# Softcap attention and a maxout feed-forward on one core: the third quad left whole, another pairing of row halves, three tiles of exponentials, and a new written order

## The chip, the core and the metric

The kernel runs on one core of one Trainium2 chip. A core has five engines with a queue of instructions each: TensorE (PE, matrix products into the accumulator memory PSUM, with a separate stream PEld for its weight loads), ScalarE (ACT, functions by element), VectorE (DVE, elementwise work and copies), GpSimd (POOL, which here issues nearly all loads) and SyncE (SP, which issues the transposing copies and most stores). Engines wait for each other through semaphores; within one queue nothing overtakes. The metric is the time of one execution on the device in microseconds (us).

## The reference

Eight batches of twelve heads of attention over 448 tokens with head width 64; scores are squeezed by a tanh before the softmax. The heads' outputs are put side by side to 3584 tokens of 768 features, and go through two products, their maximum, and a third product.

```python
scores = scale * np.matmul(q, k.transpose(0, 1, 3, 2))      # (8, 12, 448, 448)
scores = cap * np.tanh(scores / cap)
scores = scores - np.max(scores, axis=-1, keepdims=True)
attn = np.exp(scores)
attn = attn / (np.sum(attn, axis=-1, keepdims=True) + 1e-09)
x = np.matmul(attn, v)                                       # then (3584, 768)
h1 = x @ w1                                                  # w1, w2: 768 x 1024
h2 = x @ w2
return np.maximum(h1, h2) @ w_out                            # w_out: 1024 x 768
```

## The kernel before, in words

**Attention by quads.** Four heads (two rows of two heads) make a quad; there are 24, three to a batch, numbered from 0. Rows are numbered 0 to 47, two to a quad. For a quad, PE makes the scores with the 448 keys on the partitions (three blocks of 128 keys, j = 0 to 2, for each row o and head h; step `S`, line 439) and the 64 left-over keys of all four heads together (step `L`, line 457). A score step fills one of two PSUM tiles z (`s0`, `s1`), two heads at a time; ACT takes it out with a tanh into a tile of exponentials in bf16 (steps `T`, line 448, and `TL`, line 463) and then applies the exponential in place, several blocks at a time (step `E`, line 470). Row 0 of a quad has its blocks in a tile `e0`, row 1 and the left-over keys in a tile `e1`; there are EB = 2 of each kind. PE multiplies exponentials with values (`VL` line 530 for the left-over keys, `V` line 540, two steps u of 12 matmuls) into one of the two PSUM tiles s. The sums over keys come from a product with ones (`Y`): for the first three quads straight from the exponentials (lines 498 and 500, 16 matmuls), for the others after DVE has added the blocks (`A` line 480, `B` line 485), with 4 matmuls (line 503). DVE inverts the sums (`Yi`, three steps, lines 510 to 516) and normalizes (`N`, lines 555 and 559) into xT, the transposed input of the feed-forward, which also frees the PSUM tile.

**Feed-forward.** max(a, b) = relu(a - b) + b, so the kernel uses wd = w1 - w2 (six DVE subtractions, step `sub`, line 324) and a premultiplied wm = w2 @ w_out, made on PE in 12 groups at the start (`W` and `WC` turn w2 first). For each batch stage 1 makes g = relu(x wd) in 8 groups of 6 matmuls (evicted by DVE, line 614), and stage 2 makes out = x wm + g w_out for blocks of 128 tokens in two halves of 384 columns, 14 matmuls a group (evicted at line 649 and stored from there). Groups are numbered in order: 12 of premultiplication, then batch by batch.

**Row halves.** A group's matmul over 128 rows is split into two of 64 rows; two groups x and y run side by side, x on rows 0 to 63 and y on rows 64 to 127 (step `M x y n`, line 583), and change places later. Before a group changes halves, DVE has to pass it on with an empty instruction that waits for its last matmul (step `H`, line 591), since both halves write the same PSUM bank. Where y or x is -1, the other half runs alone; where x = y, full matmuls are used (line 578), as in the whole end of the kernel. A group's PSUM bank is one of four (`O`), and is freed by its eviction (`ev`).

**Cut.** In before, quad 2 is divided by queries into 256 and 192 columns (`SPLIT = (2,)`), so there are 25 items of attention rather than 24 (items 2 and 3 are quad 2, item 4 is quad 3, and so on), and stage 1 of batch 0 is made in two passes of 8 groups, 256 and 192 columns wide.

**What sets the order.** Nothing is planned at build time: a text, ORDER, lists every step, and each engine gets its instructions in that order. So one list sets all five queues. Loads (`lk`, `lq`, `lv`, `lw1`, `lw2`, `lwo`, lines 278 to 321) go through POOL; `cr` (line 374) is the transposing copy of a quad's q and k on SP from quad 5 on (before that PE transposes the rows, `X`, and DVE copies them out, `XC`); `st` stores; `D b n` issues n matmuls on a zero tile that are never read (line 337).

Of the kernel before, what the change touches and what calls it, by code (L numbers as in the profile page):

```python
# [14 lines left out]
T 1 0; E 1 1 0 2; M 1 0 4; ev 1; lq 4 0; X 4 2; XC 4; ev 0; Y 0 1; Yi 0 1; lw2 1; W 3 0; WC 3; W 2 2; WC 2; lv 0 3;
VL 0 1; lv 0 0; lv 0 1; V 0 0; V 0 1; Yi 0 2; Yi 0 3; N 0 0; N 0 1; S 2 0 0; T 2 0; E 1 1 2 4; E 1 0 0 3; O 2 3;
O 3 1; M 2 3 8; H 3; H 2; lw2 2; W 4 0; W 5 2; WC 4; WC 5; M 3 2 8; ev 3; lv 2 2; lv 1 0; lq 5 0; lv 1 3; lk 5 0;
X 5 0; O 4 2; O 5 1; M 4 5 4; XC 5; L 2 0; TL 2; M 4 5 1; S 2 2 1; T 2 2; ev 2; lw1 0; sub 1 0; M 4 5 3; H 5; S 2 1 0;
T 2 1; E 2 1 0 2; sub 0 0; Y 1 0; Yi 1 1; H 4; Yi 1 2; Yi 1 3; lv 1 1; lv 1 2; VL 1 1; V 1 0; V 1 1; N 1 0; N 1 1;
S 3 0 0; T 3 0; E 2 1 2 4; M 5 4 8; ev 4; lwo 1 0; O 6 3; O 7 0; M 6 7 1; S 3 2 0; T 3 2; M 6 7 2; lwo 1 1; M 6 7 5;  # L20
H 6; H 7; S 3 1 1; T 3 1; lk 6 0; lq 6 0; X 6 2; XC 6; ev 5; L 3 0; TL 3; E 3 1 0 2; M 7 6 8; ev 7; S 4 1 1; O 8 2;
O 9 1; M 8 9 1; S 4 0 0; T 4 0; T 4 1; lw1 1; sub 2 0; M 8 9 7; H 9; H 8; S 4 2 0; T 4 2; E 4 0 0 3; sub 3 0; ev 6;
M 9 8 8; ev 9; lv 2 1; lk 7 0; lk 8 0; lq 7 0; lq 8 0; lv 2 0; X 8 0; XC 8; ev 8; X 7 3; XC 7; lv 2 3; VL 2 1; Y 2 1;
Yi 2 1; Yi 2 2; Yi 2 3; lw1 2; sub 4 0; lk 10 0; lk 10 1; lk 9 0; lq 9 0; lq 10 0; lk 11 0; lk 11 1; lq 11 0; lk 12 0;
cr 5; lk 12 1; lq 12 0; lv 3 1; lv 3 0; lk 13 0; lv 3 2; S 5 0 0; T 5 0; O 10 0; O 11 2; M 10 11 3; V 2 0; V 2 1;
N 2 0; L 4 0; M 10 11 5; H 10; H 11; E 3 1 2 4; Y 3 3; TL 4; N 2 1; M 11 10 1; S 4 5 0; T 4 5; lv 3 3; lk 13 1;
lq 13 0; cr 6; lv 4 0; lv 4 1; lv 4 2; lv 4 3; M 11 10 4; S 4 4 1; T 4 4; M 11 10 3; S 5 1 0; T 5 1; X 9 1; S 5 2 1;
T 5 2; sub 5 0; ev 10; Yi 3 1; Yi 3 2; ev 11; O 13 0; M 13 -1 2; O 14 3; M 13 14 4; Yi 3 3; H 13; S 4 3 0; T 4 3;
E 4 1 0 2; O 17 2; M 17 14 2; M 17 13 4; H 14; M 14 13 1; XC 9; A 4 0 1; H 17; M 14 13 1; ev 13; VL 3 1; V 3 0; V 3 1;
N 3 0; N 3 1; S 5 5 0; T 5 5; M 14 17 4; ev 14; O 15 1; M 15 17 2; O 19 0; M 15 19 4; H 15; lk 14 0; lk 14 1; lq 14 0;  # L30
lk 15 0; lk 15 1; lq 15 0; lv 5 0; lv 5 1; lv 5 2; lv 5 3; lk 16 0; lk 16 1; lq 16 0; lk 17 0; lk 17 1; L 5 1; cr 7;
A 4 1 1; O 12 3; M 12 19 2; H 19; M 12 15 3; ev 17; M 12 15 1; M 19 15 1; H 12; M 19 15 1; ev 15; S 5 3 0; M 19 12 4;
ev 19; M -1 12 1; O 18 2; M 18 12 1; O 16 1; M 18 16 1; ev 12; M 18 16 4; H 18; M -1 16 1; H 16; E 4 1 2 4; B 4 0;
B 4 1; A 4 1 2; TL 5; T 5 3; E 5 0 0 3; S 5 4 1; T 5 4; E 5 1 0 2; M -1 18 1; M 16 18 5; ev 18; A 4 0 2; O 22 0;
M 16 22 1; O 20 3; M 20 22 1; ev 16; A 5 0 1; M 20 22 5; VL 4 0; V 4 0; V 4 1; Y 4 2; Yi 4 1; Yi 4 2; Yi 4 3;
M 20 22 2; L 6 1; TL 6; M 20 22 5; H 22; O 21 1; M 20 21 1; M -1 21 1; M 22 21 4; S 6 5 1; M 22 21 8; N 4 0; N 4 1;
# [700 lines left out]
```

## Time and profile before

| | us |
|---|---|
| time, median of 3 runs (329.39 to 330.75) | 329.54 |
| the profiled execution, whole | 329.36 |
| its span | 327.6 |
| PE busy | 318.0 |
| ACT busy | 273.3 |
| DVE busy | 244.8 |
| first matmul starts | 0.99 |
| first tanh starts | 6.33 |
| last tanh or exponential ends | 288.0 |
| last matmul ends (last eviction begins) | 323.4 |

The busy time of PE is the union of its matmuls, whose ends are modelled, so a busy PE may still wait for less than a matmul's length. Durations below are taken by starts where instructions follow each other.

### The profile page before, as it was taken

The page shows a single profiled execution, that of the slowest core. Times are in us where ns is not written, and L with a number is a line of the kernel's source. Part 1 is how long each engine was busy: PE and PEld are TensorE (multiplying, and loading weights), DVE is VectorE, ACT ScalarE, POOL GpSimd, SP SyncE. Part 2 cuts the span into 40 slices and gives each one's busy share as a digit, 9 for nine tenths or more (in the row PEclk, how much of TensorE's full clock was granted, in tenths as well). Part 3 has the DMA queues.
Part 4 walks back from the last instruction along what each step waited for, and adds up shares of the span by engine and source line. Part 5 has one row for each costly group of instructions (what it writes and reads, how often), then busy time and mean ns, then how long its engine had stood idle before and what let it go on. Part 6 is the DMA issues. An engine that isn't in the chain of part 4 may idle for free.

```text
span 327.6 us, 10011 instructions
## 1 busy us (share of the span) xinstructions
PE 318.0 (97%) x4288; PEld 195.1 (60%) x4288; DVE 244.8 (75%) x446; ACT 273.3 (83%) x244; POOL 164.2 (50%) x243
## 2 busy tenths in 40 slices
PE   7699999999999999999999999999999999999994
PEld 6455567576555655655665565675567667655552
DVE  2339798989877887987888778878789775995422
ACT  4998999999999999999999998999899988710000
POOL 8546699997796885565576386542202000000000
PEclk9799999999999999999999999999999999999999
DMA  8999999999999999999999999995953042004006
GB/s 152 199 223 234 270 187 159 154 173 196 169 155 183 152 125 185 184 133 165 148 193 118 145 151 212 161 87 95 189 123 46 2 115 79 3 2 144 2 0 192
DMA packets 135083, 45.90 MB, mean 140 GB/s; under 512 B 116224, under 2 KB 130688, under 8 KB 134656
## 3 DMA queue, kind: packets, MB, share of 16 engines
q0 software_dynamic: 95456, 25.08, 76.7%
q1 hardware_dynamic: 39040, 19.18, 29.7%
q10 hardware_dynamic: 544, 1.02, 0.9%
q8 instruction: 33, 0.54, 0.7%
q14 instruction: 10, 0.08, 0.1%
HBM read 47.45 MB, written 11.01 MB: 178 GB/s over the span
## 4 chain that ended last, share of the span: by engine, by line
PE 89%; ACT 8%; issue 1%; DVE 0%; DVEq 0%
PE mm L583 56%; PE s L540 8%; PE mm L578 8%; PE s L439 8%; ACT e L448 5%; ACT e L470 3%; PE s L530 2%; PE s L457 2%; PE mm L503 1%; PE mm L337 1%; PE mm L366 1%; PE mm L498 1%; PE mm L345 1%; ACT e L463 0%; DVE qkT L371 0%
## 5 line engine op out<-in xcount | busy, mean ns | idle before, releaser
L470 ACT ACTIVATE e<-e 128x1792 bf16<-128x1792 bf16 (+4 forms) x73 | 140.7, 1937 | 0.3
L448 ACT ACTIVATE e<-s 128x896 bf16<-128x896 f32 (+2 forms) x144 | 123.9, 933 | 10.7 <-PE s L439 10.6
L583 PE MATMUL mm<-wo_sb,gT 64*128 64x384 bf16 x768 | 96.2, 323 | 0.0
L583 PE MATMUL mm<-xT,wd_sb 64*128 64x448 bf16 (+2 forms) x768 | 80.1, 326 | 0.0
L583 PE MATMUL mm<-wm_sb,xT 64*128 64x384 bf16 x576 | 77.2, 323 | 0.0
L583 PEld LDWEIGHTS <-gT 64*128 64x128 bf16 x768 | 49.0, 94 | 22.6 <-issue 2.4
L303 POOL DMA_DIRECT2D vp<-in_v_dram x48 | 30.4, 637 | 61.1 <-PE mm L503 30.0
L583 PEld LDWEIGHTS <-wd_sb 64*128 64x128 bf16 x768 | 46.7, 94 | 19.8 <-issue 2.9
L285 POOL DMA_DIRECT2D kqs<-in_k_dram x76 | 54.5, 720 | 6.7 <-DMA vp<-in_v_dram 4.2
L439 PE MATMUL s<-qkT 64*128 64x448 bf16 (+2 forms) x300 | 53.7, 346 | 2.9 <-ACT e L448 1.6
L583 PEld LDWEIGHTS <-xT 64*128 64x128 bf16 x576 | 38.9, 94 | 16.6 <-issue 2.2
L614 DVE TENSOR_SCALAR gT<-mm 128x448 bf16<-128x448 f32 (+2 forms) x72 | 39.2, 567 | 10.2 <-PE mm L583 5.6
L649 DVE COPY osb<-mm 128x384 f32<-128x384 f32 x54 | 29.2, 552 | 19.3 <-PE mm L578 10.4
L285 POOL DMA_DIRECT2D kqs<-in_q_dram x38 | 34.9, 920 | 3.1 <-DMA vp<-in_v_dram 1.5
L540 PE MATMUL s<-e,vp 128*32 128x448 bf16 (+2 forms) x600 | 32.5, 347 | 0.0
L303 POOL DMA_DIRECT2D vl<-in_v_dram x48 | 29.2, 617 | 5.4 <-DMA gT<-in_moe_w_dram 4.1
L559 DVE TENSOR_TENSOR xT<-s,inv 64x448 bf16<-64x448 f32 (+2 forms) x50 | 30.2, 604 | 2.2 <-PE mm L583 1.2
L439 PEld LDWEIGHTS <-qkT 64*128 64x128 bf16 x300 | 20.8, 94 | 17.4 <-issue 5.3
L480 DVE TENSOR_TENSOR esum<-e 128x896 bf16<-128x896 bf16 x42 | 25.6, 616 | 4.9 <-PE mm L583 2.7
L485 DVE TENSOR_TENSOR esum<-esum,e 64x896 bf16<-64x896 bf16 x42 | 26.0, 619 | 3.1 <-PE mm L583 1.4
L480 DVE TENSOR_TENSOR esum<-esum,e 128x896 bf16<-128x896 bf16 x42 | 25.5, 622 | 3.1 <-PE mm L583 2.1
L463 ACT ACTIVATE e<-s 128x896 bf16<-128x896 f32 (+2 forms) x25 | 22.5, 900 | 0.8 <-PE s L457 0.4
(54 smaller groups left out, 254.5 us busy)
## 6 DMA issues: line engine op xcount, KB each, us to landing
out_dram<-osb SPq DMA_DIRECT2D x51, 192.0 KB, 4.3
vp<-in_v_dram POOLq DMA_DIRECT2D x38, 160.0 KB, 4.8
kqs<-in_q_dram POOLq DMA_DIRECT2D x47, 112.0 KB, 5.4
kqs<-in_k_dram POOLq DMA_DIRECT2D x76, 56.0 KB, 4.7
osb<-in_moe_w_dram POOLq DMA_DIRECT2D x2, 1024.0 KB, 9.0
gT<-in_moe_w_dram POOLq DMA_DIRECT2D x3, 512.0 KB, 9.8
wo_sb<-in_moe_w_out_dram POOLq DMA_DIRECT2D x4, 384.0 KB, 7.6
w1l<-in_moe_w_dram POOLq DMA_DIRECT2D x1, 1024.0 KB, 5.4
```

The lines of the kernel that those rows point to most:

```text
L285: nc.gpsimd.dma_start(out=to, in_=x)
L303: nc.gpsimd.dma_start(out=to, in_=x)
L439: nc.tensor.matmul(ps[:, h, x * w : (x + 1) * w], k_of(t, o, h, j), q_of(n, o, h))
L448: nc.scalar.activation(e, slots[n, s][:, :, :m], AF.Tanh, scale=scale / cap)
L470: nc.scalar.activation(e[:, j0 * m : hi], e[:, j0 * m : hi], AF.Exp, scale=float(cap))
L480: nc.vector.tensor_add(d, e[:, 0:2, :] if j == 1 else d, e[:, 2 * j : 2 * j + 2, :])
L540: nc.tensor.matmul(vals[n][R32[m], u, :w], vp[t % VB][:, x, j if turned_by_pe(t) else 2 * j, u::2], e_of(n, o, h, j), start=False, stop=(j ...
L559: nc.vector.tensor_mul(x[to], vals[n][r, 1, :w], sums[n, 3][to, :w])
L578: nc.tensor.matmul(self.ps, w, x, start=first, stop=self.at[0] == self.n)
L583: ins = nc.tensor.matmul(self.ps, w[r], x[r], start=first, stop=self.at == [self.n, self.n]).ins
L614: nc.vector.tensor_relu(gT[b // 2][:, f, cs], ps)
L649: nc.vector.tensor_copy(o[:, hs], ps)
```

## The change

Two constants and the order. SPLIT is empty, so quad 2 is treated as the others, with items numbered like quads, and stage 1 of batch 0 has 8 groups of 448 columns; its groups are numbered 12 to 25 rather than 12 to 33. EB is 3: three tiles e0 and three tiles e1. ORDER is another text throughout: other loads first, other pairs of groups, other places for every step. The number of `D` matmuls goes from 48 to 80. The functions are unchanged; all line numbers are six lower.

```diff
-    EB = 2
+    EB = 3
-    SPLIT = (2,)
+    SPLIT = ()
```

The order's first part, before and after (the rest differs as much):

```diff
-ld0 k; ld0 q; dm; ms0; D 0 32; cd k; cd q; lq 3 0; id; Xh 0 0 1; XC 0 0; Xh 0 1 0; XC 0 1; ms; S 0 2 0; T 0 2;
-S 0 0 1; T 0 0; S 0 1 0; T 0 1; E 0 0 0 3; lk 1 0; lq 1 0; lq 2 0; X 1 2; XC 1; S 0 3 1; S 0 4 0; T 0 4; T 0 3;
...
+lq 1 0; ld0 k; lk 1 0; dm; ms0; cd k; lw2 0; D 0 32; id; Xh 0 0 0; XC 0 0; ld0 q; cd q; Xh 0 1 1; XC 0 1; ms; S 0 1 0;
+T 0 1; S 0 0 1; T 0 0; S 0 2 0; T 0 2; E 0 0 0 3; X 1 2; XC 1; S 0 4 1; T 0 4; S 0 3 0; T 0 3; E 0 1 0 2; D 3 8;
+W 1 3; D 0 8; L 0 1; TL 0; S 0 5 0; T 0 5; E 0 1 2 4; W 0 0; lv 2 3; lv 0 2; lv 0 3; lk 3 0; lwo 0 0; lq 2 0; lv 3 3;
+lk 2 0; X 2 1; WC 0; XC 2; lq 3 0; X 3 2; XC 3; S 1 1 1; T 1 1; S 1 0 0; D 0 8; T 1 0; lk 4 0; lq 4 0; X 4 0; D 1 8;
+L 1 1; TL 1; XC 4; S 2 0 0; T 2 0; lw2 1; W 2 1; WC 1; WC 2; S 1 4 1; T 1 4; Y 0 2; S 2 2 0; T 2 2; D 0 8; S 2 1 1;
+T 2 1; O 0 0; O 1 3; M 0 1 3; S 1 3 0; T 1 3; E 1 1 0 2; M 0 1 1; lwo 0 1; M 0 1 4; Yi 0 1; H 1; S 1 5 1; T 1 5;
+W 3 1; S 1 2 0; T 1 2; E 1 1 2 4; E 1 0 0 3; H 0; M 1 0 8; WC 3; O 2 2; O 3 1; M 2 3 3; ev 0; ev 1; M 2 3 5; H 2;
+lw2 2; lk 5 0; lv 1 2; lv 1 0; lq 5 0; lv 1 1; X 5 0; XC 5; W 4 3; WC 4; Yi 0 2; VL 0 1; S 2 5 0; T 2 5; lv 0 0;
+lv 0 1; lk 6 0; V 0 0; V 0 1; Yi 0 3; N 0 0; N 0 1; H 3; W 5 0; WC 5; D 3 8; Y 1 3; Yi 1 1; Yi 1 2; E 2 0 0 3;
+S 2 4 0; M 3 2 3; S 2 3 1; T 2 3; M 3 2 5; ev 2; ev 3; O 4 0; O 5 3; M 4 5 8; lk 9 0; lq 8 0; lq 6 0; X 6 2; lk 10 0;
+lw1 0; sub 1 0; L 2 1; T 2 4; E 2 1 0 2; TL 2; E 2 1 2 4; lv 1 3; VL 1 0; V 1 0; V 1 1; H 5; H 4; XC 6; Yi 1 3; N 1 0;
+N 1 1; M 5 4 8; lwo 1 0; lk 8 0; ev 4; O 6 1; O 7 2; M 6 7 1; S 3 0 1; T 3 0; M 6 7 3; S 3 2 0; T 3 2; lwo 1 1;
+M 6 7 4; ev 5; H 6; H 7; lk 7 0; lq 7 0; X 7 0; XC 7; lw1 2; sub 5 0; lq 9 0; S 3 1 1; T 3 1; lw1 1; lk 10 1; lq 10 0;
+lk 11 0; lv 3 2; lk 11 1; lq 11 0; lv 2 0; lv 2 2; cr 5; lk 12 0; lv 2 1; lk 12 1; lq 12 0; lk 13 0; lk 13 1; lq 13 0;
+lv 4 0; lv 4 1; lv 4 2; lv 4 3; lv 3 1; lv 3 0; lk 14 0; lk 14 1; M 7 6 5; S 3 5 0; T 3 5; M 7 6 3; ev 6; L 3 1; cr 6;
+TL 3; sub 0 0; X 9 3; XC 9; ev 7; S 3 3 0; T 3 3; O 8 0; O 9 1; M 8 9 3; S 3 4 1; T 3 4; M 8 9 5; H 8; H 9; S 4 4 0;
+T 4 4; sub 2 0; X 8 3; XC 8; sub 4 0; S 4 3 1; T 4 3; M 9 8 2; S 4 5 0; T 4 5; M 9 8 5; S 4 2 1; T 4 2; M 9 8 1; ev 9;
+ev 8; sub 3 0; O 10 2; O 11 3; M 10 11 8; Y 2 1; H 11; H 10; lq 14 0; lk 15 0; lk 15 1; lq 15 0; lv 5 0; lv 5 1;
+lv 5 2; L 4 0; cr 7; VL 2 1; Yi 2 1; Yi 2 2; Yi 2 3; V 2 0; V 2 1; N 2 0; N 2 1; lv 5 3; lk 16 0; lk 16 1; lq 16 0;
+lk 17 0; lk 17 1; lq 17 0; lv 6 0; M 11 10 8; ev 11; O 12 0; O 15 1; M 12 15 6; H 12; H 15; ev 10; E 3 1 0 2;
```

In before the three thirds of w1 (`lw1 0`, `lw1 1`, `lw1 2`) are asked for as POOL's loads 23, 30 and 38; in after `lw1 0` is load 30, `lw1 2` load 37 and `lw1 1` load 39. On SP, quads 13 and 14, and 21 and 22, change places.

More of the change, by code (lines that the diff above doesn't have):

```diff
@@ L15 @@
[L15 to L24, printed above, removed]
@@ new lines @@
+S 6 0 0; T 6 0; ev 17; M 21 22 2; ev 19; M 21 22 1; O 23 3; M 21 23 1; S 5 0 1; T 5 0; A 4 1 2; M 21 23 1; H 22;
+M 22 23 3; S 5 2 0; T 5 2; E 5 1 0 2; M 22 23 2; VL 4 1; B 4 0; B 4 1; Y 4 0; V 4 0; V 4 1; Yi 4 1; Yi 4 2; H 21;
+Yi 4 3; S 6 1 0; T 6 1; M 22 23 6; A 5 1 1; N 4 0; M 22 23 1; M 22 21 1; H 23; M 22 21 1; S 6 5 0; N 4 1; ev 22;
+M 23 21 12; O 20 0; M 23 20 2; O 25 1; M 25 20 1; S 6 4 1; M 25 20 3; E 5 0 0 3; ev 21; A 5 0 1; A 5 0 2; T 6 5;
+E 5 1 2 4; T 6 4; M 25 20 8; O 24 2; M 25 24 1; H 20; S 6 2 0; T 6 2; E 6 0 0 3; B 5 1; A 5 1 2; M 25 24 1; M 20 24 4;
@@ new lines @@
+O 26 3; M 26 32 4; H 32; A 6 1 1; O 31 0; M 26 31 2; H 26; M 32 31 1; B 6 0; M 32 31 3; M 32 26 1; H 31; B 6 1;
+M 32 26 1; ev 32; S 8 3 1; T 8 3; M 31 26 3; S 8 1 0; T 8 1; E 7 1 0 2; M 31 26 1; A 6 1 2; M 31 -1 1; O 33 1;
+M 31 33 1; O 30 2; M 30 33 1; ev 31; ev 26; M 30 33 2; lv 6 1; lv 6 2; lv 6 3; VL 6 1; lk 18 0; lk 18 1; lq 18 0;
+L 8 0; TL 8; lk 19 0; lk 19 1; lq 19 0; cr 9; E 7 0 0 3; Y 6 0; Yi 6 1; Yi 6 2; Yi 6 3; V 6 0; V 6 1; M 30 33 2;
+M 30 -1 1; H 33; H 30; S 8 0 0; T 8 0; E 7 1 2 4; N 6 0; N 6 1; A 7 1 1; M 33 -1 1; M 33 30 5; O 34 3; M 34 30 1;
@@ new lines @@
+VL 8 0; lv 10 3; lk 26 0; lk 26 1; lq 26 0; lk 27 0; lk 27 1; lq 27 0; lv 11 0; lv 11 1; lv 11 2; lv 11 3; lk 28 0;
+lk 28 1; lq 28 0; lk 29 0; Y 8 3; Yi 8 1; Yi 8 2; V 8 0; V 8 1; TL 11; Yi 8 3; N 8 0; N 8 1; lk 29 1; lq 29 0;
+lv 12 0; lv 12 1; lv 12 2; lv 12 3; lk 30 0; lk 30 1; M 36 37 1; O 40 1; M 36 40 12; H 36; S 11 5 1; O 44 3;
+M 44 40 2; M 44 36 1; ev 37; H 40; E 9 1 0 2; A 9 1 1; T 11 5; M 44 36 3; M 40 36 1; S 11 0 0; M 40 36 1; S 10 5 1;
+A 9 0 1; A 9 0 2; H 44; E 9 1 2 4; A 9 1 2; T 11 0; T 10 5; M 40 36 8; ev 36; st 1 4; M 40 44 4; ev 40; O 42 2;
@@ new lines @@
+ev 45; A 10 1 1; M 43 49 1; S 11 4 1; T 11 4; E 10 1 2 4; M 43 49 3; ev 43; O 53 3; M 53 49 1; S 12 1 0; T 12 1;
+M 53 49 1; O 51 0; M 53 51 1; ev 49; M 53 51 1; S 12 2 1; T 12 2; E 11 1 0 2; M 53 51 9; A 10 0 2; M 53 51 1; O 52 2;
+M 52 51 2; VL 10 0; V 10 0; V 10 1; B 10 1; B 10 0; A 10 1 2; Y 10 1; S 12 0 1; T 12 0; H 53; M 52 53 12; H 51;
+Yi 10 1; M 51 53 2; E 11 1 2 4; E 11 0 0 3; S 12 3 1; T 12 3; E 12 1 0 2; E 12 0 0 3; Yi 10 2; Yi 10 3; A 11 1 1;
+H 52; M 51 52 2; cr 14; st 1 6; ev 53; N 10 0; N 10 1; M 51 52 10; st 1 3; ev 51; O 55 1; M 55 52 2; O 54 3;
@@ new lines @@
+M 61 62 5; ev 62; A 13 0 1; O 66 2; M 61 66 1; O 68 1; M 68 66 2; ev 61; A 13 1 1; B 13 0; S 14 3 1; T 14 3;
+M 68 66 4; S 14 0 0; T 14 0; M -1 66 1; M 68 66 2; S 14 4 1; T 14 4; M 68 66 4; H 66; S 15 5 0; T 15 5; O 64 3;
+M 68 64 2; A 13 0 2; H 68; M 66 64 1; B 13 1; A 13 1 2; M 66 64 2; S 15 2 1; T 15 2; M 66 64 3; S 14 2 0; T 14 2;
+E 14 0 0 3; M 66 64 6; M 66 68 2; ev 66; lv 13 2; lv 13 3; VL 13 1; lk 32 0; lk 32 1; lq 32 0; L 14 0; TL 14; Y 13 0;
+Yi 13 1; H 64; Yi 13 2; Yi 13 3; V 13 0; V 13 1; N 13 0; N 13 1; M 64 68 12; ev 68; S 15 4 0; O 70 2; M 64 70 2;
@@ new lines @@
+ev 64; O 71 0; M 71 70 3; E 14 1 0 2; A 14 1 1; T 15 4; S 15 0 1; T 15 0; M 71 70 3; S 15 1 0; T 15 1; M 71 70 6;
+H 70; A 14 0 1; A 14 0 2; O 69 1; M 71 69 2; lk 33 0; lk 33 1; lq 33 0; lv 14 0; L 15 1; cr 16; L 16 0; lv 14 1;
+lv 14 2; lv 14 3; lk 34 0; lk 34 1; lq 34 0; lk 35 0; lk 35 1; lq 35 0; cr 17; lv 15 0; lv 15 1; lv 15 2; lv 15 3;
+lk 36 0; lk 36 1; lq 36 0; lk 37 0; lk 37 1; lq 37 0; lv 16 0; E 14 1 2 4; A 14 1 2; H 71; TL 16; TL 15; M 70 69 12;
+H 69; S 16 3 0; T 16 3; M 70 71 2; M 69 71 2; S 15 3 1; T 15 3; E 15 0 0 3; M 69 71 3; VL 14 0; B 14 0; B 14 1;
@@ new lines @@
+M 79 76 2; O 73 2; M 79 73 1; H 76; E 16 1 0 2; T 17 5; E 16 1 2 4; N 15 1; M 79 73 1; S 17 1 1; T 17 1; M 76 73 4;
+O 78 3; M 76 78 2; S 18 1 0; T 18 1; H 73; M 73 78 3; S 18 2 1; T 18 2; M 73 78 1; ev 76; H 79; M 73 79 1; H 78;
+M 73 79 1; S 17 3 0; T 17 3; M 78 79 3; S 18 5 1; T 18 5; M 78 79 1; O 83 0; M 78 83 1; A 16 0 1; ev 73; A 16 1 1;
+B 16 1; M 78 83 1; ev 78; O 84 2; M 84 83 1; ev 79; S 17 0 0; T 17 0; M 84 83 4; S 17 2 1; T 17 2; E 17 0 0 3;
+M 84 83 2; A 16 1 2; A 16 0 2; M 84 83 5; H 83; B 16 0; O 82 3; M 84 82 2; H 84; L 18 0; TL 18; VL 16 1; V 16 0;
@@ new lines @@
+O 114 0; M 114 115 2; O 110 3; M 114 110 1; A 23 0 2; ev 115; M 114 110 11; H 114; O 113 1; M 113 110 2; M 113 114 12;
+E 23 1 2 4; A 23 1 2; B 23 1; H 110; M 110 114 2; B 23 0; N 22 1; VL 23 0; H 113; Y 23 2; Yi 23 1; Yi 23 2; Yi 23 3;
+V 23 0; V 23 1; N 23 0; N 23 1; M 110 113 4; M -1 113 2; M 110 113 8; ev 110; st 6 0; O 116 2; M 116 116 6; ev 116;
+ev 113; O 117 3; M 117 117 6; O 118 2; M 118 118 6; ev 117; ev 118; O 119 1; M 119 119 6; ev 119; O 120 3;
+M 120 120 6; ev 120; O 121 2; M 121 121 6; O 122 1; M 122 122 6; ev 122; O 123 3; M 123 123 6; ev 121; ev 123;
```

222 lines of the change are left out of this document (84 added, 138 removed).

## The prediction

> **What bounds the kernel now.** Five views, in this order. First the page: busy shares, and the slices.
>
> ```profile
> PE 318.0 (97%) x4288; PEld 195.1 (60%) x4288; DVE 244.8 (75%) x446; ACT 273.3 (83%) x244; POOL 164.2 (50%) x243
> ...
> PE   7699999999999999999999999999999999999994
> ...
> PEclk9799999999999999999999999999999999999999
> ...
> PE 89%; ACT 8%; issue 1%; DVE 0%; DVEq 0%
> ```
>
> PE is the bound from the third slice on; ACT's 8% of the chain can only lie early. Second, stretches of the span (engine sums, clock, DMA):
>
> ```profile
> 5.26:8.68 3.42, 1.65 (x42) 0.96 (x38) 1.40 (x7) 2.35 (x3) 3.42 (x6) 1.00 1.26 191
> 8.68:12.09 3.41, 3.15 (x67) 2.36 (x68) 1.38 (x3) 3.38 (x4) 1.96 (x5) 0.50 1.11 186
> 12.09:17.00 4.91, 2.96 (x41) 1.93 (x40) 1.36 (x3) 4.88 (x7) 2.03 (x4) 1.00 1.27 209
> 17.00:31.50 14.50, 14.28 (x249) 8.37 (x248) 9.32 (x17) 13.33 (x13) 8.58 (x15) 1.00 1.21 226
> 31.50:50.00 18.50, 18.50 (x362) 11.14 (x358) 16.43 (x27) 17.82 (x19) 14.05 (x21) 1.00 1.41 225
> ```
>
> PE idles visibly only before 17 us. ACT starts at 6.33 and is full from then on. Third, ACT's waits:
>
> ```profile
> ACT e L448 <- PE s L439: 10.6, 15, 1.9
> ```
>
> Those are waits for scores; none is for a tile of exponentials. Fourth, the longest piece of the chain (start, us), and four rows of PE's timeline, for the price of a matmul:
>
> ```profile
> 296.02 27.40 PE mm L578 x160
> ```
>
> ```profile
> 54.02 1.26 PE L583 MATMUL mm<-xT,wd_sb 64*128 64x256 bf16 x20
> 55.20 0.38 PE L457 MATMUL s<-qkT 64*32 64x448 bf16 x8
> ...
> 69.99 1.88 PE L583 MATMUL mm<-xT,wd_sb 64*128 64x192 bf16 x36
> 71.87 0.37 PE L439 MATMUL s<-qkT 64*128 64x448 bf16 x2
> ```
>
> The 160 matmuls of the end (48 of 448 columns, 84 of 384, 14 of 512, 14 of 256: 64,512 columns) take 27.40 us, 0.425 ns a column. Below, a slot is one full matmul, or a pair on the two row halves; by starts in the timeline it costs 0.189 us at 448 columns, 0.163 at 384, 0.110 at 256, 0.087 at 192. The rows above show the short ones dearer in place: 18 pairs of 192 in 1.88 us (0.104), 10 of 256 in 1.18 (0.118). A half alone (-1 in a step) costs a whole slot. Fifth, where before stood at two moments:
>
> ```profile
> 32.26 0.75 PE L498 MATMUL mm<-e,ones 128*32 128x448 bf16 x12
> ...
> 323.44 0.42 DVE osb L652
> ```
>
> By slots the order before holds 311.6 us of PE work, 23.9 of it ahead of the sums of quad 1 (32.26). So PE, which starts at 0.99, idled 7.35 us before that point, and 323.44 - 32.26 - 287.7 = 3.5 us after it: 2.2 until 74.0 us (the second values of quad 4, with 63.5 us of slots ahead of them) and 1.3 in the 249 us that follow. Little is left to gain after 74. Around the work: 4.1 us from the last matmul's end to the span's end, and 1.8 between the span and the execution's 329.36 us, which lies 0.2 under the median of 329.54.
>
> **The change, part by part.**
>
> *No cut.* Stage 1 of batch 0 loses 45 pairs of 256, 45 of 192, one and three mixed with 384, and 8 lone halves; it gains 48 pairs of 448 and two of 384: 45 x 0.110 + 45 x 0.087 + 4 x 0.163 + 5 x 0.110 + 3 x 0.087 = 10.3 against 48 x 0.189 + 2 x 0.163 = 9.4, so 0.9 less. The attention of that quad has the same columns in fewer matmuls: 0.13 less over scores, sums and values. On ACT six tanh of 0.80 to 1.02 become six of 0.93, 0.1 less in all: nothing. DVE loses eight evictions (8 x 0.42 + 8 x 0.36 = 6.1 become 8 x 0.62 = 5.0) and one chain of sums.
>
> *New pairs.* Lone halves fall from 24 to 16, those eight being the cut's, counted above; pairs of unequal width from 49 to 45, likewise. The rest is renumbering: nothing, and hidden by nothing, as the slots are the same.
>
> *Three tiles of each kind.* No ACT wait was for one, so by itself 0; it only permits the order. A loss would need the second tile to have been free later, which a third cannot cause; a gain is bounded by ACT's 10.6 us of waits, nearly all after 130 us, when PE is the bound anyway.
>
> *The new order, to 32 us.* Warm matmuls go from 48 to 80. Eight cost 0.55 us on the chain, so +2.2 (no less than 1.8, at 56 ns each as the transposes of w2 run). They stand where PE waits for ACT: two score tiles, each freed only by its tanh. The first point that pins PE is the sums of quad 1 (Y 1), which need its last exponentials. Ahead of those ACT has 15 tanh x 0.81, 2 leftover tanh x 0.81 and two quads of exponentials (2.4 + 1.6 + 1.6 each): 25.0 us. From 6.33, and with 0.25 for what the same sum misses before (it gives 24.2 with a gap of 0.75, the trace 24.46), Y 1 can start at 31.6. Ahead of it PE has 23.4 us of slots, 6.9 of them warm: idle 31.6 - 0.99 - 23.4 = 7.2, as before. Behind it 289.35 us remain; before, at the same instant, 288.4 remained. So the new order is 1.0 us behind there, although its useful work is 1.05 less in all.
>
> *From 32 to 74 us.* Before idles 2.2. Of that the short pairs' excess over the prices used is 45 x 0.017 + 45 x 0.008 = 1.1, which goes. New: stage 1 of batch 0 can't begin on 256 columns; its fifth pair waits for xT of the whole third quad. PE gets there at 31.6 + 46.1 - 23.4 + 0.3 = 54.6. DVE, from the copy of row 7's transposes (42.1), has five subtractions (1.22), two copies (0.62), four wm evictions (0.55), the inversion (0.65 + 0.24 + 0.65) and the normalization (0.62 + 1.24): 12.9, so xT at 55.0, and with 0.2 for the handover PE waits 0.6. Idle here 2.2 - 1.1 + 0.6 = 1.7 (bounds 0 and 2.8).
>
> *Loads.* Weights of w1 move behind more rows. POOL waited until 37.73 for the second third of w1 when 12.4 MB of source had been asked for, 0.37 MB/us from 4.0 on. In the new order the last two thirds complete 13.7 and 14.95 MB: 41 and 44.4 us, needed at 42.1 and 46.4. Cost 0 with 1 to 2 us of cover; without it each us late is a us on xT above. Eight loads in flight, as before. At the start two row loads and a third of w2 are now issued ahead of the identity on POOL (0.57 us each, from 1.24): identity at 3.3 us, needed at 4.5, so 0. The SP queue has the same 19 transposes; quads 13/14 and 21/22 swap there, each still a quad ahead of its scores by the chain's 11 us a quad: 0.
>
> *From 74 us on.* Idle stays 1.3: nothing in the trace separates the orders there (bounds 0.7 and 2). The last 27.4 us are the same matmuls.
>
> Sum: 31.6 + 289.35 + 1.7 + 1.3 = 323.95, plus 4.1 and 1.8: 329.85, half a us over the profiled execution; I take 329.8, the median plus 0.3.
>
> **Clock.** The granted clock was 0.50 for 3.41 us after a stretch with PE busy 1.65 of 3.42, and stayed at 1.00 after one busy 2.96 of 4.91. In the new order the stretch 12 to 17 us holds 3.1 us of slots (leftover and two scores, half of w2, rows 2 and 3, 8 warm), about as before, so no second half-rate stretch is in the sum. *TensorE: Matmul & The Clock Gate* of the Trainium skill, section "What's actually happening", says that the array's clock is gated to half by default and after an idle window of about 3.4 us; by that rule, the 3.41 us row agrees, a late load at 14 us would bring a second such window.
>
> **Rivals.** (1) *Faster: the idle of 32 to 74 us was the cut's altogether.* For it: H handovers come every 6 short pairs, every 0.5 us; against it: xT's wait is new. Idle there 0, and 1.0 later: 31.6 + 289.35 + 1.0 + 5.9 = 327.85. (2) *Slower: w1 lands late.* Its thirds took 8.0 and 10.1 us to land before; the new order issues two of them close together. The 5 subtractions stand in front of the inversion of quad 2 on DVE, and all PE work left is stage 1. From 46.4 each us costs one; at 48.5 the time is 329.8 + 2.1 = 331.9, and past 1.4 us late it is slower by 0.5%. Against it: the 0.37 MB/us held over 33 us. (3) *A second window at half clock* between 12 and 19 us: up to 3.41/2 = 1.7 us of PE, of which the 7.2 us idle absorb half: 330.7. (4) *The third tile and the order do nothing*: 329.5; inside the forecast's range.
>
> **How the numbers follow.** Forecast with (4) 0.56, its own range 328.6 to 330.9; (1) 0.17; (2) 0.20; (3) 0.07. 0.5% is 1.65 us, about what a measurement of this kernel can tell: the bounds are 327.9 and 331.2. Faster: most of (1) and a little of the forecast, 0.15. Slower: (2), some of (3) and the forecast's edge, 0.23. Same 0.62. The range, from (1) to (2): 327.6 to 332.0.
>
> **What would show it.** PE matmuls 4156; the sums of quad 1 starting within 0.4 us of 31.6 (earlier: the pin is wrong); first 448-wide stage-1 pairs near 54, with a gap of about 0.6 after four pairs; idle later near 3 us; ACT ending between 286 and 291; the end stretch again 27.4 us. DVE waiting on a DMA into osb or w1l between 42 and 50 would be rival 2; a clock row under 1 after 12 us rival 3. A PE wait on qkT from SP, which I cost at nothing, would break the forecast.

## The result and the profile after

The changed kernel takes 337.08 us in the median of five runs (331.77 to 337.29), before 329.54 (329.32 to 330.75, five runs): 7.5 us or 2.3% more by the medians. The interval given for the ratio, 1.0107 (1.0061 to 1.0153), goes by the two shortest of the five runs alone, 331.77 and 335.02; only one of the other three was traced, so what made these two shorter is not shown. The profiled execution took 337.09 with a span of 335.3, as three of the five did. The forecast was 329.8, with a range to 332.0: wrong by 7.3 us against this execution, and the median of the five lies outside the range.

The page of the changed kernel: busy time, PE and its clock by slices of 8.4 us, and the chain by engine.

```profile
PE 321.5 (96%) x4156; PEld 188.3 (56%) x4156; DVE 243.9 (73%) x432; ACT 275.1 (82%) x242; POOL 164.4 (49%) x243
...
PE   7789999999995999999999999999999999999994
...
PEclk9799999999997899999999999999999999999998
...
PE 85%; ACT 6%; DMA 4%; DVE 3%; issue 1%; DVEq 0%
```

PE is still the bound, but slice 13 (100.6 to 109.0 us) is half empty, the clock row has a dip there that before has not, and the chain holds 4% of DMA, where before it held none. Stretches around that place, first after, then before (length, busy us of PE, PEld, DVE, ACT, POOL, granted clock, DMA share, GB/s):

```profile
99.00:102.55 3.55, 3.55 (x41) 2.67 (x39) 3.12 (x6) 3.55 (x4) 1.38 (x2) 1.00 1.71 165
102.55:104.91 2.36, 0.33 (x4) 0.00 (x0) 1.51 (x3) 2.36 (x3) 0.65 (x1) 1.00 1.97 109
104.91:111.74 6.83, 5.12 (x32) 2.43 (x34) 2.40 (x4) 3.32 (x3) 4.89 (x8) 0.50 1.47 151
111.74:116.00 4.26, 4.26 (x70) 1.96 (x68) 2.96 (x6) 2.60 (x3) 3.01 (x4) 1.00 1.83 171
```

```profile
104.91:111.74 6.83, 6.83 (x104) 4.02 (x106) 5.52 (x11) 6.83 (x5) 5.96 (x10) 1.00 1.79 162
```

In the same 6.83 us before issued 104 matmuls, after 32. PE's timeline and the chain show what PE waited for:

```profile
102.23 0.65 PE L577 MATMUL mm<-wo_sb,gT 64*128 64x384 bf16 x5
106.62 0.56 PE L433 MATMUL s<-qkT 64*128 64x448 bf16 x2 [3.75 <-DMA qkT<-kqs]
```

```profile
92.72 0.33 PE mm L577 x4
93.05 13.53 DMA qkT<-kqs
106.58 0.05 issue
106.62 0.56 PE s L433 x2
```

The first scores of quad 9 (step `S 9 5 0`) wait for the transposing copy of that quad. It is issued at 93.05 and lands 13.5 us later, at 106.58. SP's timeline of after shows what stands ahead of it, and of the two copies behind it:

```profile
83.30 9.46 SPq L624 DMA_DIRECT2D out_dram<-osb  x6
93.05 16.05 SPq L368 DMA_TRANSPOSE qkT<-kqs  x3
```

Those six are the stores of batch 0 (tile 1 at 83.3; tiles 2 and 0, four pieces of 192 KB, at 89.9 to 91.7, when their evictions are through). In before the copies stood between the stores, at 81.17, 92.45 and 103.62.

The price: PE idles for 3.9 us (102.55 to 106.62 without the 0.16 of a slot), and then does 5.12 us of the stretch at half clock, half of which, 2.56, is lost by my estimate. Together that is about 6.5 us. The traces bear it out: from the sums of quad 1 to the last matmul's end the changed kernel takes 298.33 us, and 291.89 in the experiment below in which the stores are spread, 6.44 less. The rest of the kernel is within a microsecond of the forecast. The last 160 matmuls take 27.65 us (303.00 to 330.65), before 27.4.

### The profile page after: what moved, and what is told of

It reads as the page before. It is cut to its first block, busy times and chain, and to the rows that moved or that the text cites. A ratio compares the mean times of both kernels' runs of the same rounds, so it can differ in the third digit from the quotient of the medians.

```text
span 335.3 us, 9727 instructions
## 1 busy us (share of the span) xinstructions
PE 321.5 (96%) x4156; PEld 188.3 (56%) x4156; DVE 243.9 (73%) x432; ACT 275.1 (82%) x242; POOL 164.4 (49%) x243
## 4 chain that ended last, share of the span: by engine, by line
PE 85%; ACT 6%; DMA 4%; DVE 3%; issue 1%; DVEq 0%
PE mm L577 52%; PE s L433 9%; PE mm L572 8%; PE s L534 7%; DMA qkT<-kqs 4%; ACT e L464 3%; ACT e L442 2%; PE s L451 2%; PE s L524 2%; PE mm L497 1%; PE mm L331 1%; PE mm L360 1%; DVE xT L553 1%; DVE esum L474 1%; PE mm L339 1%; PE mm L492 1%
## 5 line engine op out<-in xcount | busy, mean ns | idle before, releaser
L464 ACT ACTIVATE e<-e 128x1792 bf16<-128x1792 bf16 (+1 forms) x72 | 139.7, 1954 | 0.6
L442 ACT ACTIVATE e<-s 128x896 bf16<-128x896 f32 x144 | 124.5, 930 | 11.6 <-PE s L433 11.4
L577 PE MATMUL mm<-wo_sb,gT 64*128 64x384 bf16 x768 | 97.3, 327 | 0.0
L577 PE MATMUL mm<-wm_sb,xT 64*128 64x384 bf16 x576 | 79.8, 327 | 0.0
L577 PE MATMUL mm<-xT,wd_sb 64*128 64x448 bf16 x672 | 78.3, 349 | 0.0
L433 PE MATMUL s<-qkT 64*128 64x448 bf16 x288 | 54.3, 355 | 7.4 <-DMA qkT<-kqs 3.7
L577 PEld LDWEIGHTS <-wd_sb 64*128 64x128 bf16 x672 | 41.2, 94 | 24.0 <-issue 2.5
L608 DVE TENSOR_SCALAR gT<-mm 128x448 bf16<-128x448 f32 x64 | 38.1, 618 | 6.0 <-PE mm L572 3.4
L433 PEld LDWEIGHTS <-qkT 64*128 64x128 bf16 x288 | 19.1, 94 | 23.8 <-issue 7.9
L474 DVE TENSOR_TENSOR esum<-e 128x896 bf16<-128x896 bf16 x42 | 25.7, 617 | 8.4 <-PE mm L577 7.4
L534 PE MATMUL s<-e,vp 128*32 128x448 bf16 x576 | 31.7, 353 | 0.0
L553 DVE TENSOR_TENSOR xT<-s,inv 64x448 bf16<-64x448 f32 x48 | 29.9, 622 | 1.3 <-PE s L433 0.3
L457 ACT ACTIVATE e<-s 128x896 bf16<-128x896 f32 x24 | 21.9, 919 | 6.5 <-PE s L451 6.5
```

The source lines that it names most:

```text
L433: nc.tensor.matmul(ps[:, h, x * w : (x + 1) * w], k_of(t, o, h, j), q_of(n, o, h))
L442: nc.scalar.activation(e, slots[n, s][:, :, :m], AF.Tanh, scale=scale / cap)
L464: nc.scalar.activation(e[:, j0 * m : hi], e[:, j0 * m : hi], AF.Exp, scale=float(cap))
L474: nc.vector.tensor_add(d, e[:, 0:2, :] if j == 1 else d, e[:, 2 * j : 2 * j + 2, :])
L534: nc.tensor.matmul(vals[n][R32[m], u, :w], vp[t % VB][:, x, j if turned_by_pe(t) else 2 * j, u::2], e_of(n, o, h, j), start=False, stop=(j ...
L553: nc.vector.tensor_mul(x[to], vals[n][r, 1, :w], sums[n, 3][to, :w])
```

## The experiments

**Stores behind the copy.** Theory T blames SP's order. The edit to the changed kernel takes the three stores from their places and sets them behind `cr 9`:

```diff
-... ev 23; st 0 1; M 20 24 8; ...
-... ev 24; st 0 2; st 0 0; S 7 3 0; ...
-... lk 19 1; lq 19 0; cr 9; E 7 0 0 3; ...
+... ev 23; M 20 24 8; ...
+... ev 24; S 7 3 0; ...
+... lk 19 1; lq 19 0; cr 9; st 0 1; st 0 2; st 0 0; E 7 0 0 3; ...
```

> The changed kernel with one edit: the three stores of batch 0 stand behind the transposing copy of quad 9 in SP's queue, not ahead of it. Theory T (the time was lost because that copy issued 12 us late, at 93.05 instead of about 81, and two more followed at its heels): it issues at 81 to 82, lands in 5 to 8 us, PE has no wait on qkT at 102 to 107, the granted clock stays at 1.00 after 12 us, and the span falls by the 4.1 us of idle and the 3.4 us of the half-rate stretch to 327.5 to 328.5: 329.3 to 330.3 us, the same as the kernel before. Rival R1 (the uncut third quad and the late work of w1 cost the time, and the wait at 102 only shows slack that another wait would show): the wait moves, and the time stays above 334. Rival R2 (the clock falls for reasons of its own in this order): no wait on qkT, but a half-rate stretch remains somewhere after 12 us, 333 us.

Measured: 330.81 us (330.2 to 331.89), ratio to before 1.0041 (1.0026 to 1.0056). PE has no wait between 100 and 112 us, and the granted clock is full from 13.7 us on. T holds so far, and R1 and R2 fall: three steps moved in the list give back 6.3 us of the profiled execution's 337.09. The span is 329.0, 0.5 to 1.5 more than I expected; 0.8 of that is the half clock, which I had counted with 3.4 us where it cost 2.56. The landing time of two copies in this kernel, quad 9's at 82.2 and quad 10's at 92.8, shows something more:

```profile
L368 SPq DMA_TRANSPOSE qkT<-kqs x1: 1610/1610/1610, 82.2 to 82.2; - x1
...
DMA to landing us min/median/max: 4.9/4.9/4.9
```

```profile
L368 SPq DMA_TRANSPOSE qkT<-kqs x1: 4057/4057/4057, 92.8 to 92.8; - x1
...
DMA to landing us min/median/max: 13.4/13.4/13.4
```

The second one is as slow as quad 9's was, only that nobody waits for it.

**One copy at a time.** The changed kernel with a dependency added, so that the copy of quad 10 waits.

```diff
+        if t in held:          # held = {10: (8, 4)}
+            tc.add_manual_dep(ins.ins, score_ins[held[t]].name, BANK, reason="hold")
```

> The changed kernel with SP's queue as it is (the copy of quad 9 behind the stores, at 93.05), but the copy of quad 10 held back until the score matmuls of step S 8 4 are done (101.9), so that no second copy starts behind the first for 8.8 us. If the long landing (13.5 us, where single copies took 5.2 to 10.0) is due to the copies that follow at once (T, second half): quad 9's lands at 99 to 101, ahead of its first use at 102.5, and the time is 329.5 to 331. If the four stores just ahead of it or the loads of GpSimd make it slow (rival R3), or lateness alone does: it still lands near 106, and the time is 336 to 337.

Measured: 333.95 us (332.44 to 336.59), ratio 1.0158 (1.0116 to 1.0200). In the profiled execution, of 332.56, the copy of quad 9 lands after 11.7 us although it is alone, and PE waits for it:

```profile
104.67 0.36 PE L437 MATMUL s<-qkT 64*128 64x448 bf16 x2 [1.59 <-DMA qkT<-kqs]
```

So the long landing does not need copies behind it; that half of T falls, and R3 (stores or loads) stands. The 1.8 us between 11.7 and 13.5 may be the copies behind or may be chance, as the next run has 9.4 with the changed kernel's own queue. The gap here is 1.92 us from pair to pair (102.75 to 104.67), and no half-rate stretch follows. The two longer executions, 335.33 and 336.59, were not traced.

**The waiting step later.**

```diff
-... lv 7 0; S 9 5 0; T 9 5; lv 7 1; ...
+... lv 7 0; lv 7 1; ...
-... M 38 34 2; L 9 1; TL 9; ...
+... M 38 34 2; S 9 5 0; T 9 5; L 9 1; TL 9; ...
```

> The changed kernel with its queues of copies as they are, but the first score step of quad 9 moved 21 matmul slots (3.4 us) later on PE, right ahead of that quad's leftover scores. The copy lands at 106.6 as before. T: PE works through most of the wait, idles at most 1 us at 105.9, and the clock does not fall, so that both prices go together: 329.5 to 331. R2 (clock of its own): the half-rate stretch stays, 333. R1: 335 or more.

Measured: 333.24 us (332.38 to 334.72), ratio 1.0116 (1.0093 to 1.0140). There is no wait for qkT, and the clock is full from 100 us on, as T says; but the run does not test T. The copy did not land at 106.6: issued at 94.38, behind the same four pieces and with the same copies behind it, it landed after 9.4 us, at 103.8. PE comes by the old place of the step at about 104.6, so it would not have waited there either. And the time is 2 us more than T expects. Most of the excess stands early in the profiled run. PE's clock fell for a second time (21.30 to 24.72), and the sums of quad 1 start 28.1 us after the first tanh (34.35 and 6.23), where the changed kernel has 25.7. Later ACT got the moved tile of scores late, and PE waits 0.83 us for ACT at 110. The stretches around the early fall of the clock:

```profile
14.48:21.30 6.82, 4.82 (x126) 3.59 (x124) 2.98 (x5) 6.63 (x8) 3.54 (x7) 1.00 1.06 164
21.30:24.72 3.42, 3.42 (x30) 1.45 (x28) 1.34 (x2) 1.61 (x2) 0.93 (x2) 0.50 1.18 197
```

The order up to 100 us is that of the changed kernel, so this second half-rate stretch can come with the new order too; it was seen in this one profile. What the run does show is that one and the same queue of stores and copies gave landings of 9.4 and of 13.5 us.

**Before with a late copy.**

```diff
-... E 6 1 0 2; L 7 1; cr 9; TL 7; ...
+... E 6 1 0 2; L 7 1; TL 7; ...
-... B 7 0; S 8 4 0; T 8 4; ...
+... B 7 0; S 8 4 0; cr 9; T 8 4; ...      # held = {9: (8, 4)}
```

> The kernel before, with the copy of quad 9 taken from its place (81.2) to behind the store of tile 2 and held until the score matmuls of step S 8 4 (101.6); its first use is at 104.8. T: it lands at 107 to 115, PE idles 3 to 10 us at 104.8 (more if the next copy, at 103.6, slows it to 13 us), and after an idle of over 3.4 us a half-rate stretch of about 6.8 us costs another 3.4: 335 to 343. R1 (a late copy alone is covered by the rest of the work): within 1.5 us of 329.5.

I had misread the numbers: with the cut, item 8 of before is quad 7, so the hold was over early, and the copy went out when SP came to it, at 95.1. The run tests what it should all the same. Measured: 335.04 us (333.67 to 335.63), ratio 1.016 (1.014 to 1.018). SP, and then the stretch, in this run:

```profile
93.74 1.23 SPq L633 DMA_DIRECT2D out_dram<-osb  x2
95.13 11.88 SPq L376 DMA_TRANSPOSE qkT<-kqs  x2
```

```profile
104.50:107.19 2.69, 0.27 (x3) 0.00 (x0) 1.40 (x3) 2.47 (x2) 1.69 (x3) 1.00 1.67 130
107.19:114.01 6.82, 5.67 (x58) 2.13 (x60) 0.77 (x2) 2.31 (x2) 5.95 (x10) 0.50 1.83 187
```

It lands after 13.2 us, with two pieces just ahead of it and quad 10's copy, issued at 89.97, still under way. PE waits from 104.5 to 108.3, and the clock halves for the same 6.8 us. One copy moved behind stores makes the old kernel 5.5 us slower; R1 falls here too.

**As late, but with no store ahead.** What made the copies slow, the stores (T2) or GpSimd's loads (R3)? In the changed kernel the stores of tiles 2 and 0 go behind `cr 9`, which is held to its old time.

```diff
-... ev 24; st 0 2; st 0 0; S 7 3 0; ...
-... lq 19 0; cr 9; E 7 0 0 3; ...
+... ev 24; S 7 3 0; ...
+... lq 19 0; cr 9; st 0 2; st 0 0; E 7 0 0 3; ...   # held = {9: (7, 5)}
```

> The changed kernel with the copy of quad 9 as late as it was (held until the score matmuls of step S 7 5, about 92.7), but with the stores of tiles 2 and 0 of batch 0 behind it in SP's queue. Theory T2 (a transposing copy shares a queue with the stores, and the four pieces of 192 KB issued in the 3 us ahead of it are what made quad 9's take 13.5 and 11.7 us, and quad 10's 13.4 in the kernel with the stores behind): it lands in 5 to 8 us, at 98 to 101, ahead of its use at 102.5; quad 10's, now right behind the four pieces, takes 12 to 14 but is needed at about 112 only. No wait of PE on quad 9's, clock at 1.00 after 12 us, 330 to 332 us. Rival R3 (the loads of GpSimd in flight at 92 to 106 make it slow): it takes 11 to 13.5 us all the same, PE waits 2 to 4 us, 333 to 337. Rival R4 (lateness alone, at any landing): 335 to 337.

Measured: 330.64 us (330.42 to 331.16), ratio 1.0027 (1.0008 to 1.0046). SP's queue, and the landing of the copy issued at 92.7 and of that at 98.0:

```profile
92.73 2.19 SPq L370 DMA_TRANSPOSE qkT<-kqs  x1
95.02 2.78 SPq L627 DMA_DIRECT2D out_dram<-osb  x4
98.04 11.26 SPq L370 DMA_TRANSPOSE qkT<-kqs  x2
```

```profile
DMA to landing us min/median/max: 6.4/6.4/6.4
```

```profile
DMA to landing us min/median/max: 13.4/13.4/13.4
```

The copy moves with the stores: as late as in the changed kernel, it lands in 6.4 us without them and PE does not wait; the next, behind the four pieces, takes 13.4. R4 falls, and so does R3 as the whole cause, since the loads are those of the changed kernel. Lateness alone costs nothing here; late and slow together do.

**Stores spread.**

```diff
-cr 9; E 7 0 0 3; ... cr 10; lv 8 2; ...
+cr 9; st 0 1; E 7 0 0 3; ... cr 10; st 0 2; st 0 0; lv 8 2; ...   (and taken from their old places)
```

> The changed kernel with the stores of batch 0 spread: tile 1's behind the copy of quad 9, tiles 2's and 0's behind that of quad 10. T2: quad 9's copy lands in 5 us (82 to 87) as with all three behind it, and quad 10's, at 92.5 with no store in the 8 us ahead of it, in 6 to 8 us where it took 13.4; quad 11's, behind four pieces, may be the slow one. R3: quad 10's still takes 11 to 13. Neither is waited for, so by both the time is that of the kernel with all stores behind, 330.8 within 0.5.

Measured: 330.61 us (330.41 to 332.12), ratio 1.0031 (1.0012 to 1.0049). Quad 10's copy, issued at 92.7 as in the first experiment, now lands in 6.5 us:

```profile
L368 SPq DMA_TRANSPOSE qkT<-kqs x1: 2272/2272/2272, 92.7 to 92.7; - x1
...
DMA to landing us min/median/max: 6.5/6.5/6.5
```

Only the stores moved, GpSimd's queue is the same. T2 holds for these copies. Quad 11's, issued at 102.2, 5.3 us after the last of the four pieces, is not slow either: 6.2 us. Copies by the pieces of stores that SP issued in the 4 us ahead of them, and by whether another copy was still under way:

| kernel, quad, issued at | pieces ahead | us to landing |
|---|---|---|
| stores behind, 9, 82.2 | 0 | 4.9 |
| late without stores, 9, 92.7 | 0 | 6.4 |
| stores spread, 9, 82.0 and 10, 92.7 | 0 | 6.5, 6.5 |
| before with a late copy, 10, 90.0 | 2 | 9.4 |
| step later, 9, 94.4 | 4 | 9.4 |
| one copy at a time, 9, 92.9 | 4 | 11.7 |
| late without stores, 10, 98.0 | 4, a copy under way | 13.4 |
| stores behind, 10, 92.8 | 4 | 13.4 |
| changed kernel, 9, 93.0 | 4 | 13.5 |
| before with a late copy, 9, 95.1 | 2, a copy under way | 13.2 |
| changed kernel, 10, 97.3 and 11, 103.4 | 0, copies under way | 12.9, 11.4 |
| one copy at a time, 10, 102.5 | 0, a copy under way | 5.2 |

At this point of the kernel, issued at 92 to 98 us, the copies with none ahead and no copy under way took 5.4 to 8.4 us (6.4 and 6.5 here, and 6.9, 8.4 and 5.4 in the three later variants of the kernel with the stores spread), and those behind four pieces 9.4 to 13.5. So by these copies the stores cost 1 to 8 us here; that is no price for every copy. Later in the changed kernel copies behind four pieces took 7.8, 7.2 and 6.3 us (issued at 169.6, 203.0 and 238.6), and one with none ahead 3.4 (253.1), so the loads may set part of it. Nor are the bounds sharp: in the kernel before with three tiles (below) a copy with none ahead took 8.8 at 83.1, and in the try with useful work for warm matmuls (below) quad 11's, with none in the 4 us ahead but stores still under way, took 11.7.

*DMA: Bandwidth & Descriptors* of the Trainium skill, section "Queues, rings and completion order", says that SP's transfers share one row of rings, each of which is worked off in order; the table agrees in that copies are later behind stores. The order alone gives less than was measured: the stores of the changed kernel had landed by 98.3 (the last issued at 91.65, 6.7 us at most), and 6.4 more would be 104.7, not 106.6. Where the last 1.9 come from stays open; the two copies behind are one candidate.

**Without 48 of the 80 warm matmuls**, from the kernel with the stores spread. They feed nothing.

```diff
-E 0 1 0 2; D 3 8; W 1 3; D 0 8; L 0 1; ... S 1 0 0; D 0 8; ... X 4 0; D 1 8; ... T 2 2; D 0 8; ... WC 5; D 3 8; Y 1 3;
+E 0 1 0 2; W 1 3; L 0 1; ... S 1 0 0; ... X 4 0; ... T 2 2; ... WC 5; Y 1 3;
```

> The kernel with the stores spread, with only the first 32 of its 80 warm matmuls. Those feed nothing: the output is the same. The forecast had the other 48 hidden, because the sums of quad 1 are pinned by ScalarE; in the trace of the changed kernel they start 0.7 us later than that (32.32 for 31.6), right behind eight warm ones (31.65 to 32.27), while the exponentials they need end at about 32.1. If the pin is ScalarE: the sums start at 32.0 to 32.3, and the time falls by 0 to 0.3 us against the kernel with the stores spread. If the warm matmuls are on the path (they stand in the chain twice, 0.55 and 0.46): the sums start at 31.3 and the time falls by 1.0. If they are there for the clock: PE is idle for longer between 9 and 19 us, the clock row falls below 1 for 3.4 us or more in that stretch, and the time rises by 0.5 to 2.

Measured: 332.01 us (330.26 to 332.92), ratio to before 1.0060 (1.0039 to 1.0080), 1.4 slower than with them by the medians. The profiled execution took 330.9. PE's timeline with its wait, and the stretch in which the clock is half:

```profile
31.79 0.75 PE L492 MATMUL mm<-e,ones 128*32 128x448 bf16 x12 [0.54 <-ACT e L464]
```

```profile
7.56:17.80 10.24, 8.20 (x146) 5.43 (x145) 2.56 (x4) 10.14 (x10) 6.99 (x13) 0.50 1.20 176
```

One of the three theories holds: the sums of quad 1 are pinned by ACT. PE now waits for them, and they start 25.6 us after the first tanh (6.18), as they do with the warm matmuls (25.7). The theory of the clock fits the longer time, but the traces do not bear it out. The clock row of the kernel with the stores spread shows no fall only because it has no record before 12.9 us: eight warm matmuls at 10.76 take 1.04 us there, and eight at 17.08 take 0.62, so that kernel too ran at half rate there, until about 12.9.

```profile
10.76 1.04 PE L331 MATMUL mm<-warm 128*128 128x128 bf16 x8
17.08 0.62 PE L331 MATMUL mm<-warm 128*128 128x128 bf16 x8
```

And the half clock did not delay the sums: they start 0.7 us earlier than in that kernel's profile (31.79 and 32.50). What is lost stands behind them, 0.8 us of 292.7, in waits such as 0.27 us for an eviction at 45.2 and 0.38 us for a copy at 66.4. Why the median is 1.4 us longer is not shown.

**Before with three tiles.** `EB = 2` becomes `EB = 3`.

> The kernel before with three tiles of each kind of exponentials in place of two, and nothing else. The forecast had this part at 0, as no wait of ScalarE in the trace is for a tile: within 0.5 us of 329.5. If a wait for a tile hid behind the waits for scores (10.6 us in all, nearly all of them after 130 us), it is faster by up to 1 us; if the third tiles move others to where they collide, slower.

Measured: 329.38 us (329.06 to 331.69), ratio 1.0001 (0.9982 to 1.0019): nothing, as forecast.

**Useful work for warm matmuls**, a try to beat both, from the kernel with the stores spread.

```diff
-... T 2 2; D 0 8; S 2 1 1; ...
-... WC 5; D 3 8; Y 1 3; Yi 1 1; Yi 1 2; E 2 0 0 3; S 2 4 0; M 3 2 3; S 2 3 1; T 2 3; M 3 2 5; ev 2; ...
+... T 2 2; S 2 1 1; ...
+... WC 5; M 3 2 3; M 3 2 5; Y 1 3; Yi 1 1; Yi 1 2; E 2 0 0 3; S 2 4 0; S 2 3 1; T 2 3; ev 2; ...
```

> The kernel with the stores spread, with the last two groups of eight warm matmuls (22.4 and 31.8 us, in a stretch in which PE is never idle) taken out, and the 8 pairs of 384 that stand behind the sums of quad 1 (M 3 2 3 and M 3 2 5) set right ahead of them in their place. Nothing else moves. If PE's work is the bound from 20 us on, the 1.1 us of warm matmuls come off the end: 329.5 us, the same as the kernel before within 0.3, with the sums of quad 1 at 32.5 to 32.8. If ScalarE pins the sums at 25.7 us after its first score, whatever stands ahead, and PE makes up the rest by waiting elsewhere: 330.3 to 330.6. If the warm groups keep the clock here too: a half-rate stretch after 20 us and over 331.

Measured: 330.78 us (330.18 to 332.81), ratio 1.0047 (1.0025 to 1.0069). No gain. The chain (start, us) goes through a new wait:

```profile
33.75 0.22 PE mm L494 x4
33.97 0.02 issue
34.00 0.66 DVE st L504
34.66 0.04 issue
34.70 1.46 PE mm L577 x15
```

The next pairs use the PSUM bank that DVE's transpose of the sums reads; the eight pairs had covered that step. PE idles only 0.11 us there, though, and from the first tanh to the last matmul's end it is 317.6 us as with the stores spread, so where the rest of the 1.1 us went is not shown. Hence one more try with three pairs moved (and only the last eight warm matmuls out).

```diff
-... WC 5; D 3 8; Y 1 3; ... S 2 4 0; M 3 2 3; S 2 3 1; T 2 3; M 3 2 5; ...
+... WC 5; M 3 2 3; Y 1 3; ... S 2 4 0; S 2 3 1; T 2 3; M 3 2 5; ...
```

> The kernel with the stores spread, with only the eight warm matmuls right ahead of the sums of quad 1 (31.83, 0.55 to 0.61 us) taken out, and three of the pairs behind those sums (M 3 2 3, 0.49 us) in their place; the other five pairs stay behind, where they cover VectorE's transpose of the sums (0.66 us), for which the next pairs wait. In the run with all eight pairs ahead, that cover was gone: PE's chain there goes through the transpose at 34.00, and the 1.1 us of warm matmuls taken out came to nothing. Theory P (the cover was the loss): the sums start at 32.3 to 32.5, PE does not wait for the transpose, and the last matmul ends 0.4 to 0.5 us earlier after ScalarE's first score: 330.1 to 330.2. Rival (ScalarE pins PE up to 50 us, whatever is moved between): the same distance as before, 317.6 us, and 330.6.

Measured: 330.77 us (330.41 to 333.24), ratio 1.0047 (1.0020 to 1.0073), and 318.4 us from the first tanh to the last matmul in the profiled run, where 317.6 was to be beaten. The transpose is off the chain, but in this execution the chain runs through a load of w1 that lands late:

```profile
32.79 11.15 DMA w1l<-in_moe_w_dram
43.94 0.03 issue
43.97 0.02 DVEq L318
43.99 0.05 issue
44.04 0.13 DVE wd_sb L318
```

Neither theory is decided by it. No version that I ran beats the kernel before.

## Why the prediction was wrong

The step that failed is the sentence on SP's queue: "The SP queue has the same 19 transposes; quads 13/14 and 21/22 swap there, each still a quad ahead of its scores by the chain's 11 us a quad: 0." I had looked at the copies' order among themselves and not at the stores between them, although those go through the same queue. So the term was put at 0, and it cost 6.44 us. The end of the prediction names this very wait as what would break the forecast, but no rival priced it.

The sum, against the execution of 337.09 (in us): forecast 329.85; sums of quad 1 later (32.32 for 31.6) +0.72; late copy +6.44; other idle after those sums, as with the stores spread, 2.54 for 3.0, -0.46; from the last matmul to the span's end 4.65 for 4.1, +0.55. That is 337.10.

Point by point:

- *No cut, new pairs*: 4156 matmuls, as worked out. The first pairs of 448 columns in stage 1 start at 55.14 (forecast near 54). The wait of 0.6 for xT of the third quad did not come: VectorE was through at 56.1, not 55.0, but PE had come later too, and its timeline shows no wait there.
- *Three tiles*: 0, shown by the run with that part alone.
- *The order to 32 us*: right mechanism, wrong size. ACT pins the sums of quad 1, shown by the run without the warm matmuls. But they start at 32.32, not within 0.4 of 31.6: the first tanh starts at 6.58 instead of 6.33, and ACT's operations take 25.6 us where I had 25.25. The eight warm matmuls just ahead end when ACT does, which hides them:

```profile
31.65 0.61 PE L331 MATMUL mm<-warm 128*128 128x128 bf16 x8
32.32 0.75 PE L492 MATMUL mm<-e,ones 128*32 128x448 bf16 x12
```

  So "hidden" was right for the 48 as far as these sums go: without them PE waits for ACT there. Why the median is longer without them is open. The price of 0.55 us for eight was too low for those ahead of 12.8 us, which ran at half clock: eight took 1.03 at 9.96, where the eight above took 0.61. What the sum calls idle holds that too, in both kernels.
- *Loads (rival 2)*: w1 came at its limit. VectorE waits 0.68 us for it at 43.65, which cost nothing in the changed kernel; in the last experiment's profile the same load is on the chain.
- *From 32 us to the end*: forecast idle 1.7 and 1.3. Without the late copy it is 2.5 in all, by the kernel with the stores spread, whose last matmul ends 291.89 us after the sums of quad 1 begin, 2.54 over the 289.35 of slots. The 6.44 lie in the part from 74 on, where I had seen nothing that separates the orders.
- *Clock (rival 3)*: placed wrongly. After 12 us the clock did fall, but at 104.9, behind the idle of 4.07 us from pair to pair. *TensorE: Matmul & The Clock Gate* of the Trainium skill, section "What's actually happening", which the prediction cites for 12 to 19 us, has the clock halved by an idle window of about 3.4 us; the runs agree in part. Gaps of 4.07 (changed kernel) and 3.89 us (before with a late copy) brought a half-rate stretch and the 1.92 of one copy at a time did not, but the clock fell 2.0 and 2.4 us after the last matmul had ended (102.88 and 104.77), not 3.4. The second early stretch that the rival spoke of was seen in one profile only, that of the step moved later, and there it came without such a gap: PE was busy for 1.78 of the 3.41 us ahead of it (17.89 to 21.30).
- *ACT's end*: 296.8, forecast 286 to 291; 290.5 with the stores spread.

With the copy mended the kernel takes 330.6 us, 0.8 over the forecast and 0.31% (0.12 to 0.49) over before: there is no gain in the new order here, and the forecast's other steps stand within a microsecond.

## What to carry to other kernels

A written order sets every queue at once: when it moves evictions and stores, look at what stands behind a store in its queue, and price a copy's lead as issue to landing with the stores ahead of it, not as issue to landing alone. A stall on the busiest engine may cost more than its length: here 3.9 us of idle brought 2.6 us of half clock with it. Work that looks spare at the front is not free to take out or move before it is tried: 48 warm matmuls fewer cost 1.4 us by the medians, and neither of the two tries with useful work in their place gained anything.

## What the runs showed that I had not expected

- At about 93 us of this kernel the time of a transposing copy doubles behind stores in SP's queue: 6.4 and 6.5 us with none ahead, 13.5 and 13.4 behind four pieces of 192 KB, with the same loads of GpSimd around them. The same four pieces gave 11.7 and 9.4 in two other runs.
- SP itself is held by such a copy: of the copies in the table, its instruction takes 3.2 to 6.1 us where the landing takes 9.4 or more (4.00 for quad 9 in the changed kernel), and 1.6 to 2.3 where it takes 4.9 to 6.5, so that what stands behind it in the queue is late too.
- The half-rate stretches that the clock's record holds ahead of the last matmul last 3.41, 6.83 or 10.24 us: one, two or three times the same length. They begin without 3.41 us of idle ahead: PE was busy for 1.38 us of the 3.41 ahead of 104.91 in the changed kernel, and for 0.99 ahead of 107.19 in the kernel before with a late copy.
- The row of the granted clock can be silent on the start: where it has no record before 12.9 us, the pace of the warm matmuls shows half rate.
